# Query features on eight array tiles, kv and key features on four, whole-row loads on one queue, and a new order of the first and the last chunk of a sketched attention with a two-layer block behind it

## The chip, the cores and the metric

One core of a Trainium2 chip runs the whole kernel. The metric is the time of the device in microseconds. Engines are named as in the profile: PE (TensorE; PEld its weight loads), DVE (VectorE), ACT (ScalarE), POOL (GpSimd) and SP (SyncE, which here only issues DMAs).

## The reference

The inputs are q, k, v of shape (4, 4, 1088, 32) in float32 (batch, head, row, width), two sketches S1 and S2 of shape (8, 32), and for the second block g_ln (128), w_ch1 (128, 512) and w_ch2 (512, 128). S1, S2, w_ch1 and w_ch2 are float64.

```python
def phi(x):                                  # 64 features of a row of 32
    a, b = S1 @ x, S2 @ x                    # 8 each
    return outer(a, b)
kv  = sum over s of phi(k)[s, f] * v[s, d]   # 64 x 32 for each batch and head
z   = sum over s of phi(k)[s, f]
att = (phi(q) @ kv) / (phi(q) @ z + 1e-06)
x   = the four heads side by side            # (4, 1088, 128)
xn  = (x - mean(x)) / sqrt(var(x) + 1e-06) * g_ln
out = x + max(xn @ w_ch1, 0) @ w_ch2
```

## The kernel before

All matmuls are in float32. The work is cut into nine chunks. Chunks 0 to 7 are halves of a batch, four tiles of 128 rows each; chunk 8 (`LAST`) gathers the 64 rows left over from each of the four batches, two tiles. The order of all instructions is written out by hand: each engine runs its own instructions in program order, so what stands where in the code sets the queues. All eight PSUM banks are named by number.

**Loads** (lines 100 to 143). K and Q of batch 0 come in parts (`load_rows` with a part), V of batch 0 by four loads and two small ones on ACT's queue, w1, g, w2 and everything later on SP's.

**Start** (184 to 220). Twelve matmuls of an identity with itself run on PE (191). `hm` and `hp2` are masks of ones and zeros by head. S1 and S2 are turned into float32 on DVE (`rounded`, 146, the same routine that takes a float64 weight apart into a main and a rest term: an absolute value on ACT (163), a clamp on POOL (164), four steps on DVE (169 to 174)), laid out four times side by side (213) and transposed on PE into bank 7 (217). From that come `sk` (485), 128 x 64, which holds S1 and S2 for each head on the head's own 32 partitions, and `wb` and `wa` (494), 128 x 128, for two heads at a time.

**Keys of a batch.** `key_rows` (240) transposes K on DVE in 32 x 32 blocks, in three parts (four tiles, four tiles, 64 rows). `key_features` (259) multiplies by `sk` on PE: the stationary operand is 64 rows of K at a time, so two column tiles of the array. ACT copies the result (269), and `key_products` (271) forms the 64 products of each row and head, mostly on POOL, for batch 0 in part on DVE. `key_tokens` (248) copies V beside a column of ones, which makes z a column of kv. `key_values` (283) sums phi(k) times V over nine tiles on PE, per tile four matmuls with 64 columns in the stationary operand and 33 to stream; two ACT copies (297) lay the four heads' results out in `kvz`, block by block over two heads, zeros between, which POOL writes in `fill` (222).

**Queries of a chunk.** `query_rows` (304) transposes Q on DVE. `query_features` (317) runs, for each half of the chunk, `wb` and `wa` against Q for two pairs of heads: a row tile of 64 partitions for each pair, 128 columns in the stationary operand, 256 to stream. ACT copies one factor (333), DVE multiplies the other by it (337) into `qp`. `numerators` (343) multiplies `qp` by `kvz`, 64 rows of the output at a time (32 in chunk 8), two heads at once, 66 columns to stream; DVE adds 1e-6, takes the reciprocal and multiplies (364 to 369) for each half.

**Second block.** `statistics` (379) takes mean and variance on DVE and POOL, `root` (403) the inverse root on ACT, DVE and POOL, `turn_x` (419) transposes x on PE into bank 7 with an ACT copy (427). `hidden` (429) is one quarter of the first layer: a matmul with 512 columns to stream into bank 4 or 5, then the maximum with 0 on ACT (437). `second` (439) is the second layer into bank 6, `result` (450) scales and adds on DVE (457) and stores. The first layer's weight is made on the chip: `center` (512) takes mean and g_ln into it, and `first_weight` (475) multiplies, one half of w1 at a time.

**The loop** (529). In iteration c: the four quarters of the first layer of chunk c; the inverse root of c; numerators and statistics of c + 1; in every second iteration the kv products of the next batch, in the others its key features and key products; the second layer of c; the turning of x of c + 1; the result of c; the query features of c + 2. Iteration 0 differs: the query features of chunk 1, the keys of batch 1 and the preparation of w2 stand there (534 to 545), with the statistics of chunk 0 behind POOL's key products, and the numerators of chunk 1 behind the second layer. In the last iteration the two tiles are taken one after the other, second layer and result, both through bank 6 (563 to 567).

## Time and profile before

| what | value |
|---|---|
| time, median of 3 runs | 142.17 us (141.99 to 142.64) |
| the profiled execution's own time | 142.8 us |
| its span, first to last instruction | 140.9 us |
| mean granted clock of PE | 0.949 |
| busy: PE / DVE / ACT / POOL | 122.1 / 62.7 / 46.0 / 45.7 us |
| instructions in all, of them PE matmuls | 3109, 1259 |

A float32 matmul of the program stands in the profile as two matmul instructions and two weight loads. Matmuls are pipelined and their ends are modelled, so the chain of waits, which gives each instruction only the time until the next one could follow, is the better measure of what a group of them costs. "x16" is a count of instructions. In the chain, "issue" is time in which an engine waited for nothing that the profile shows; ACTq or SPq is the queue of an engine that issues DMAs. A group's last part is the idle time before it and what ended it.

### The profile page before, as it was taken

The numbers are of one execution on the slowest core, as the hardware profiler recorded it, in microseconds if no ns is written. First come the engines' busy times: TensorE is split into PE (matmuls) and PEld (weight loads), VectorE is DVE, ScalarE is ACT, GpSimd is POOL, SyncE is SP. The second block draws the span as 40 slices with busy tenths as digits, with TensorE's granted clock in tenths as the row PEclk, the third lists the DMA queues.
The fourth block names the chain that finished last, engine by engine and source line by source line (L and its number), as shares of the span: only waits on it lengthen the run. The fifth ranks groups of instructions, "written<-read, shape, count | busy, mean of one in ns | idle before, by whom it ended". The sixth has DMA issues, their size and how long they took to land.

```text
span 140.9 us, 3109 instructions
## 1 busy us (share of the span) xinstructions
PE 122.1 (87%) x1259; PEld 90.9 (65%) x1259; DVE 62.7 (45%) x194; ACT 46.0 (33%) x100; POOL 45.7 (32%) x139
## 2 busy tenths in 40 slices
PE   6966751995399799999999999999999999999861
PEld 6955631454399555983897399479839938839650
DVE  2359553507402834733525583334336435513310
ACT  0048112275000236226214631631362263161320
POOL 5007503005797520592270039423002302304020
PEclk9999995599869869999999999999999999999998
DMA  2999989980000011002100200110020020011021
GB/s 63 245 285 352 243 265 230 305 219 0 2 0 5 0 38 39 5 0 44 37 0 7 65 7 0 27 52 0 5 56 19 0 45 34 2 34 41 6 59 51
DMA packets 8782, 10.17 MB, mean 72 GB/s; under 512 B 2112, under 2 KB 6848, under 8 KB 8768
## 3 DMA queue, kind: packets, MB, share of 16 engines
q1 hardware_dynamic: 7888, 9.41, 26.0%
q10 hardware_dynamic: 880, 0.56, 1.8%
q8 instruction: 10, 0.16, 0.5%
q14 instruction: 4, 0.03, 0.1%
HBM read 7.74 MB, written 2.23 MB: 71 GB/s over the span
## 4 chain that ended last, share of the span: by engine, by line
PE 69%; DMA 8%; POOL 8%; DVE 5%; issue 4%; ACT 2%; SPq 1%; POOLq 0%; ACTq 0%
PE banks L434 23%; PE banks L443 20%; PE banks L328 11%; PE banks L358 6%; DMA qn<-in_q_dram 4%; DMA vn<-in_v_dram 4%; POOL kp L276 3%; PE banks L290 3%; PE banks L425 2%; PE banks L479 2%; POOL cl L164 2%; PE banks L264 2%; POOL v L257 1%; SPq L106 1%; DVE x L369 1%
## 5 line engine op out<-in xcount | busy, mean ns | idle before, releaser
L443 PE MATMUL banks<-w,hT 128*128 128x128 f32 x272 | 34.6, 287 | 4.6 <-POOL w L541 3.3
L443 PEld LDWEIGHTS banks<-w,hT 128*128 128x128 f32 x272 | 32.9, 200 | 5.4 <-POOL w L541 3.4
L434 PE MATMUL banks<-xT,w 128*128 128x512 f32 (+1 forms) x72 | 33.3, 604 | 0.5 <-ACT xT L427 0.5
L437 ACT ACTIVATE hT<-banks 128x512 f32<-128x512 f32 (+1 forms) x36 | 20.7, 574 | 12.4 <-PE banks L434 12.3
L434 PEld LDWEIGHTS banks<-xT,w 128*128 128x128 f32 x72 | 12.0, 194 | 18.2 <-ACT hT L437 10.2
L276 POOL TENSOR_TENSOR kp<-fs 128x1024 f32<-128x1024 f32 (+1 forms) x10 | 16.1, 1628 | 8.4 <-ACT fs L269 8.4
L337 DVE TENSOR_TENSOR qp<-banks,qb 128x512 f32<-128x512 f32 x17 | 11.6, 689 | 15.2 <-ACT qb L333 15.2
L412 POOL TENSOR_TENSOR r<-va,r 128x4 f32<-128x4 f32 (+1 forms) x9 | 1.8, 200 | 50.7 <-DVE den L364 46.2
L457 DVE SCALAR_TENSOR_TENSOR ob<-banks,rstd,x 128x128 f32<-128x128 f32 x34 | 9.7, 343 | 18.3 <-PE banks L443 6.9
L427 ACT COPY xT<-banks 128x512 f32<-128x512 f32 (+1 forms) x9 | 5.1, 563 | 29.1 <-PE banks L425 29.1
L411 DVE RECIPROCAL r<-r 128x4 f32<-128x4 f32 (+1 forms) x9 | 1.6, 176 | 29.1 <-ACT r L407 29.1
L328 PE MATMUL banks<-qT,wb 64*128 64x256 f32 x68 | 12.0, 432 | 1.8 <-DVE qT L233 1.0
L333 ACT COPY qb<-banks 128x512 f32<-128x512 f32 x17 | 9.9, 586 | 8.4 <-PE banks L328 8.4
L358 PEld LDWEIGHTS banks<-kvz,qp 128*64 128x64 f32 (+1 forms) x288 | 8.7, 134 | 6.1 <-issue 5.3
L328 PE MATMUL banks<-qT,wa 64*128 64x256 f32 x68 | 11.1, 406 | 0.0
L290 PE MATMUL banks<-v,kp 128*64 128x33 f32 (+1 forms) x288 | 9.7, 223 | 1.2 <-POOL kp L276 0.6
L358 PE MATMUL banks<-kvz,qp 128*64 128x66 f32 (+1 forms) x288 | 9.9, 224 | 0.6 <-ACT kvz L297 0.6
L290 PEld LDWEIGHTS banks<-v,kp 128*64 128x64 f32 (+1 forms) x288 | 9.2, 137 | 1.8 <-issue 0.9
L328 PEld LDWEIGHTS banks<-qT,wb 64*128 64x128 f32 x68 | 6.2, 197 | 4.4 <-issue 1.8
L164 POOL TENSOR_SCALAR cl<-cl 128x256 f32<-128x256 f32 (+1 forms) x3 | 4.1, 1355 | 14.2 <-ACT cl L163 14.1
L328 PEld LDWEIGHTS banks<-qT,wa 64*128 64x128 f32 x68 | 7.2, 204 | 1.0
L369 DVE TENSOR_TENSOR x<-banks,rden 128x256 f32<-128x256 f32 x17 | 7.2, 424 | 0.6
(66 smaller groups left out, 111.0 us busy)
## 6 DMA issues: line engine op xcount, KB each, us to landing
out_dram<-ob SPq DMA_DIRECT2D x8, 256.0 KB
kn<-in_k_dram SPq DMA_DIRECT2D x3, 544.0 KB
qn<-in_q_dram SPq DMA_DIRECT2D x3, 544.0 KB
vn<-in_v_dram SPq DMA_DIRECT2D x12, 128.0 KB
w_raw<-in_moe_w_ch_dram SPq DMA_DIRECT2D x2, 512.0 KB
kn<-in_k_dram SPq DMA_DIRECT2D x2, 256.0 KB
vn<-in_v_dram ACTq DMA_DIRECT2D x4, 128.0 KB
qn<-in_q_dram SPq DMA_DIRECT2D x2, 256.0 KB
```

Of the source, the lines that this page charges most:

```text
L164: eng.tensor_scalar(out=size, in0=size, scalar1=2.0**-15, scalar2=_f32_of(0x47EFFFFF), op0=ALU.max, op1=ALU.min,)
L276: eng.tensor_tensor(out=_ap(kp, 0, m, t0 * H * F, [[F, tiles * H], [R, R], [1, R]]), in0=_ap(fs, 0, m, 0, [[R2, tiles * H], [1, R], [0, R] ...
L290: nc.tensor.matmul(kvp[F * (h % 2) : F * (h % 2) + F, D1 * (h // 2) : D1 * (h // 2 + 1)], kp[0:m, H * F * t + F * h : H * F * t + F * (h + ...
L328: nc.tensor.matmul(bank(2 * i2 + pair)[:, o : o + 256], w[rows, :], qT[rows, 256 * i2 : 256 * i2 + 256], start=True, stop=True,)
L333: nc.scalar.copy(_ap(qb, 0, P, 0, two), _ap(banks, 0, P, 1024 * i2, [[512, 2], [1, 256]]))
L337: nc.vector.tensor_tensor(out=_ap(p, 0, P, 0, two), in0=_ap(banks, 0, P, 1024 * i2 + 256, [[512, 2], [1, 256]]), in1=_ap(qb, 0, P, 0, two) ...
L358: nc.tensor.matmul(nd[u : u + step, o : o + 2 * D1], qp[:, t : t + step], kvz[:, 2 * D1 * pair : 2 * D1 * (pair + 1)], start=True, stop=True,)
L369: nc.vector.tensor_tensor(out=_ap(x, 0, P, 256 * i2, [[D, 2 * H], [1, D]]), in0=_ap(nd, 0, P, 0, [[D1, 2 * H], [1, D]]), in1=_ap(rden, 0, ...
L434: nc.tensor.matmul(hp[:, 0:n], w1[:, P * j : P * (j + 1)], xTs[c][:, 0:n], start=True, stop=True)
L437: nc.scalar.activation(hTs[c][:, 512 * j : 512 * j + n], hp[:, 0:n], AF.Relu)
L443: nc.tensor.matmul(po[:, DM * i : DM * (i + 1)], hT[:, 512 * j + P * i : 512 * j + P * i + P], w2[:, DM * j : DM * (j + 1)], start=(j == 0 ...
L457: nc.vector.scalar_tensor_tensor(out=ob[:, t], in0=po[:, t], scalar=rstd[:, i : i + 1], in1=x[:, t], op0=ALU.mult, op1=ALU.add,)
```

## The change

Loads: K and Q of every batch come as whole rows (4,352 bytes per partition), all on SP's queue; V of batch 0 goes from ACT's queue to SP's, behind Q of batch 0 and ahead of w1.

Array tiles: the query features work on 32 partitions (one head) and 64 columns (`wa`, `wb` without the mask), both halves of the chunk and all four heads in turn: 16 matmuls for 8. Key features take 32 rows of K in the stationary operand for 64, and the kv products 32 columns for 64: twice the matmuls each. The numerators follow the new layout: one head, 64 partitions, 33 columns to stream, 32 matmuls for 16. `kvz` loses its zeros and `fill` the writing of them; ACT makes four copies for two. DVE's denominators of a chunk are taken together.

Order of the first chunk: six warm-up matmuls for twelve; `wa` and `wb` are copied by ACT; part 1 of V's copies goes from ACT to POOL; both clamps of w1 stand ahead of `center`, w1's second half is multiplied between the second and third quarter of the first layer (bank 7); w2's clamp stands ahead of the loop; the statistics of chunk 0 go ahead of POOL's key products, and the copies of V ahead of the product of each part; the root of chunk 0 goes ahead of the second layer. In the last chunk the root stands ahead of the first layer, and the two tiles have a bank each.

```diff
-    load_rows(kn, k, 0, 0)
-    load_v(0, nc.scalar, False)
-    load_rows(kn, k, 0, 1)
-    load_rows(qn, q, 0, 0)
+    load_rows(kn, k, 0)
+    load_rows(qn, q, 0)
+    load_v(0, nc.sync, False)
+    load_v(0, nc.sync, True)
     nc.sync.dma_start(out=w1_raw, in_=moe_w_ch1)
-    load_v(0, nc.scalar, True)
...
-    for i in range(12):
+    for i in range(6):
         nc.tensor.matmul(bank(i % 2)[:, 0:P], ident, ident, start=True, stop=True)
...
     def key_features(b, part, at):
-            for u in range(0, m, 64):
+            for u in range(0, m, 32):
                 nc.tensor.matmul(
-                    kf[u : u + 64, 64 * i : 64 * i + 64],
-                    kT[:, P * i + u : P * i + u + 64], sk, start=True, stop=True,
+                    kf[u : u + 32, 64 * i : 64 * i + 64],
+                    kT[:, P * i + u : P * i + u + 32], sk, start=True, stop=True,
                 )
...
     def key_values(b, at):
-            for h in range(H):
+            for i in range(2 * H):
+                h, o = i // 2, 32 * (i % 4)
                 nc.tensor.matmul(
-                    kvp[F * (h % 2) : F * (h % 2) + F, D1 * (h // 2) : D1 * (h // 2 + 1)],
-                    kp[0:m, H * F * t + F * h : H * F * t + F * (h + 1)],
+                    kvp[o : o + 32, D1 * (h // 2) : D1 * (h // 2 + 1)],
+                    kp[0:m, H * F * t + 32 * i : H * F * t + 32 * i + 32],
                     v1[0:m, W * t + D1 * h : W * t + D1 * (h + 1)],
...
     def query_features(c):
-        for i2 in range(ntiles(c) // 2):
-            for o, w in ((0, wb), (256, wa)):
-                for pair in range(2):
-                    rows = slice(64 * pair, 64 * pair + 64)
+        for o, w in ((0, wb), (256, wa)):
+            for half in range(2):
+                for h in range(H):
+                    rows = slice(D * h, D * h + D)
                     nc.tensor.matmul(
-                        bank(2 * i2 + pair)[:, o : o + 256],
-                        w[rows, :], qT[rows, 256 * i2 : 256 * i2 + 256], start=True, stop=True,
+                        bank(h)[F * half : F * half + F, o : o + n], w[rows, :],
+                        qT[rows, n * half : n * half + n], start=True, stop=True,
                     )
...
     def numerators(c):
+        for i in range(n):
+            for h in range(H):
+                for half in range(2):
+                    rows = slice(F * half, F * half + F)
                     for u in range(0, P, step):
                         kvz = kvzs[CHUNKS[c][0] if c < LAST else u // 32]
+                        t, o = 256 * h + P * i + u, W * i + D1 * h
                         nc.tensor.matmul(
+                            bank(half)[u : u + step, o : o + D1], qp[rows, t : t + step],
+                            kvz[rows, D1 * h : D1 * h + D1], start=True, stop=True,
                         )
...
+    def second_at(c, i):
+        return bank(6)[:, DM * i : DM * (i + 1)] if c < LAST else bank(6 + i)[:, 0:DM]
...
     for c in range(LAST + 1):
         b = c // 2 + 1
+        if c == LAST:
+            root(c)
         for j in range(JC):
+            if (c, j) == (0, 2):
+                first_weight(1)
             hidden(c, j)
         if c == 0:
-            next(w2_steps)
             query_features(1)
             for part in range(3):
-                key_features(1, part, (6, 7, 3)[part])
+                key_features(1, part, (6, 7, 5)[part])
...
+            statistics(0)
             for part in range(3):
+                key_tokens(1, part, nc.gpsimd)
                 key_products(1, part, nc.gpsimd)
-                key_tokens(1, part, nc.gpsimd)
-            statistics(0)
-        root(c)
+            root(0)
+            second(0)
+            numerators(1)
+            key_values(1, 3)
...
```

## Rows read from the trace of the kernel before

**Rows 1.** Page, part 4: the chain that ended last, share of the span by engine.

```profile
PE 69%; DMA 8%; POOL 8%; DVE 5%; issue 4%; ACT 2%; SPq 1%; POOLq 0%; ACTq 0%
```

**Rows 2.** Chain in order of time, to chunk 1: start us, length us, what.

```profile
22.17 1.07 POOL cl L164
...
26.14 4.29 PE banks L434 x8
...
42.87 0.23 POOL v L257
...
44.25 0.21 POOL va L400
...
47.86 3.67 PE banks L328 x16
51.52 3.73 PE banks L434 x8
```

**Rows 3.** The same chain, steady part and last chunk: one row of each kind.

```profile
81.69 0.93 PE banks L264 x32
...
87.16 1.93 PE banks L328 x16
...
92.82 1.09 PE banks L358 x32
93.90 2.19 PE banks L290 x72
...
122.20 1.06 PE banks L328 x8
...
126.99 0.61 PE banks L358 x32
```

**Rows 4.** Timeline to 20 us: start us, length us, engine, line, what; idle before.

```profile
1.34 7.68 ACTq L116 DMA_DIRECT2D vn<-in_v_dram  x6
1.34 5.49 PE L192 MATMUL banks<-ident 128*128 128x128 f32 x24 [1.34 <-POOL ident masks.py:199]
...
3.91 0.28 DVE L213 TENSOR_TENSOR s<-up,rest 16x128 f32<-16x128 f32 x1
...
5.31 0.71 DVE L233 STREAM_TRANSPOSE kT<-kn 128x512 f32<-128x512 f32 x1 [1.13 <-DMA kn<-in_k_dram]
...
9.05 1.28 ACT L186 ACT_TABLE_LOAD   x1 [9.05 <-DMA qn<-in_q_dram]
...
11.17 2.72 POOL L276 TENSOR_TENSOR kp<-fs 128x1024 f32<-128x1024 f32 x1 [8.36 <-ACT fs L269]
...
19.86 0.70 PE L479 MATMUL banks<-rest,center 128*128 128x256 f32 x2
```

**Rows 5.** Page, part 2: GB/s of all DMA in 40 slices of 3.52 us.

```profile
GB/s 63 245 285 352 243 265 230 305 219 0 2 0 5 0 38 39 5 0 44 37 0 7 65 7 0 27 52 0 5 56 19 0 45 34 2 34 41 6 59 51
```

**Rows 6.** Groups by line and form: busy us, mean ns of one; idle before.

```profile
L257 POOL COPY v<-vn 128x512 f32<-128x512 f32 x6 | 3.6, 613 | 0.0
...
L297 ACT COPY kvz<-banks 64x66 f32<-64x66 f32 x8 | 1.7, 210 | 8.7 <-PE banks L290 6.7 <-POOL center L512 1.9
...
L164 POOL TENSOR_SCALAR cl<-cl 128x256 f32<-128x256 f32 x2 | 2.1, 1075 | 5.7 <-ACT cl L163 5.7
...
L163 ACT ACTIVATE cl<-w_raw 128x256 f32<-128x256 f32 x2 | 0.9, 439 | 0.0
```

**Rows 7.** Windows: length, busy of PE, PEld, DVE, ACT, POOL; granted clock; DMA.

```profile
16.70:18.26 1.56, 0.45 (x16) 0.31 (x12) 1.40 (x6) 0.00 (x0) 0.00 (x0) 1.00 0.99 305
20.56:21.76 1.20, 0.57 (x4) 0.19 (x2) 0.00 (x0) 0.96 (x3) 0.00 (x0) 0.57 1.10 235
20.70:27.50 6.80, 3.86 (x9) 2.12 (x8) 3.37 (x8) 1.55 (x4) 1.06 (x1) 0.50 1.08 268
```

**Rows 8.** Timeline of the end: start us, length us, engine, line; idle before.

```profile
136.60 1.16 PE L443 MATMUL banks<-w,hT 128*128 128x128 f32 x8 [1.29 <-DVE ob L457]
137.80 0.35 DVE L457 SCALAR_TENSOR_TENSOR ob<-banks,rstd,x 128x128 f32<-128x128 f32 x1 [1.25 <-PE banks L443]
```

More of the change, by code (lines that the diff above doesn't have):

```diff
@@ L98, with load_rows @@
     w2_raw = raw_tile([P, JC * DM], moe_w_ch2, "w2_raw")
-    def load_rows(t, src, b, part=None):
-        base = src.offset + b * H * S * D
-        cuts = {None: [(0, [[1, G * D]])], 0: [(0, [[256, 4], [1, 128]])],
-                1: [(128, [[256, 4], [1, 128]]), (1024, [[1, 64]])]}
-        for o, free in cuts[part]:
-            nc.sync.dma_start(
-                out=_ap(t[b], 0, P, o, free),
-                in_=bass.AP(src.tensor, base + o, [[G * D, P]] + free),
-            )
+    def load_rows(t, src, b):
+        nc.sync.dma_start(
+            out=t[b], in_=bass.AP(src.tensor, src.offset + b * H * S * D, [[G * D, P], [1, G * D]])
+        )
     def load_v(b, eng, rest):
@@ L296, in key_values @@
         for i in range(2):
-            nc.scalar.copy(
-                _ap(kvz, F * i, F, D1 * i, [[2 * D1, 2], [1, D1]]),
-                _ap(kvp, F * i, F, 0, [[D1, 2], [1, D1]]),
-            )
-    qTs, qps, xs, rs, mvs, xTs, hTs, obs = {}, {}, {}, {}, {}, {}, {}, {}
+            for to in range(2):
+                nc.scalar.copy(
+                    _ap(kvz, F * to, F, D1 * i, [[2 * D1, 2], [1, D1]]),
+                    _ap(kvp, F * i, F, 0, [[D1, 2], [1, D1]]),
+                )
+    qTs, qps, xs, rs, mvs, xTs, hTs = {}, {}, {}, {}, {}, {}, {}
     def query_rows(c):
@@ L363, in numerators @@
-            rden = small.tile([P, 2 * H], F32, tag="rden", name="rden")
-            nc.vector.tensor_scalar(
-                out=den, in0=_ap(nd, 0, P, D, [[D1, 2 * H]]),
-                scalar1=1e-6, scalar2=None, op0=ALU.add,
-            )
-            nc.vector.reciprocal(rden, den)
+                            bank(half)[u : u + step, o : o + D1], qp[rows, t : t + step],
+                            kvz[rows, D1 * h : D1 * h + D1], start=True, stop=True,
+                        )
+        den = small.tile([P, 4 * H], F32, tag="den", name="den")
@@ L369, in numerators @@
+        rden = small.tile([P, 4 * H], F32, tag="rden", name="rden")
+        m = n * H
+        nc.vector.tensor_scalar(
+            out=_ap(den, 0, P, 0, [[m, 2], [1, m]]),
+            in0=_ap(banks, 0, P, D, [[512, 2], [D1, m]]),
+            scalar1=1e-6, scalar2=None, op0=ALU.add,
+        )
+        nc.vector.reciprocal(rden[:, 0 : 2 * m], den[:, 0 : 2 * m])
+        for half in range(2):
             nc.vector.tensor_tensor(
-                out=_ap(x, 0, P, 256 * i2, [[D, 2 * H], [1, D]]),
@@ L371, in numerators @@
-                in0=_ap(nd, 0, P, 0, [[D1, 2 * H], [1, D]]),
-                in1=_ap(rden, 0, P, 0, [[1, 2 * H], [0, D]]),
+                out=_ap(x, 0, P, D * m * half, [[D, m], [1, D]]),
+                in0=_ap(banks, 0, P, 512 * half, [[D1, m], [1, D]]),
+                in1=_ap(rden, 0, P, m * half, [[1, m], [0, D]]),
                 op=ALU.mult,
@@ L475, in first_weight @@
     def first_weight(i):
-        w1p, terms = bank(4 + i), next(w1_steps[i])
+        w1p, terms = bank((4, 7)[i]), w1_terms[i]
         for j, term in enumerate(terms):
@@ L487 @@
     )
+    for w, o, pat in ((wb, R, [[0, R], [1, R]]), (wa, 0, [[1, R], [0, R]])):
+        nc.scalar.copy(_ap(w, 0, P, 0, [[R, R], [1, R]]), _ap(sp, 0, P, o, pat))
     key_rows(0, 1)
@@ L556 @@
                 key_products(b + 1, part, nc.gpsimd)
-        if c < LAST:
-            second(c, 0, 4)
-        if c == 0:
-            numerators(1)
-            statistics(1)
-            key_values(1, 3)
-        if c == LAST:
-            for i in range(ntiles(c)):
-                second(c, i, i + 1)
-                result(c, i, i + 1)
-            break
+        if c > 0:
+            second(c)
         turn_x(c + 1)
         query_rows(c + 2)
-        result(c, 0, 4)
+        result(c)
         query_features(c + 2)
```

112 lines of the change are left out of this document (47 added, 65 removed).

## The prediction

> **What bounds the kernel now.** I read the chain of waits that ended last first. TensorE (PE) carries 69% of it [rows 1], but the rest is not spread evenly. The same chain in order of time splits the span in two. Up to 51.52 us, where the hidden layer of chunk 1 starts, it hops between DMA, POOL, DVE and PE [rows 2]; from there to the numerators of the last chunk at 126.99 us [rows 3] it is PE alone. So the start must be read for what comes late, and the middle for what PE spends. In the middle one chunk is made of the pieces of [rows 3]: query features 1.93 us (16 instructions; each f32 matmul shows as two, so eight matmuls), numerators 1.09 (32 instructions), in every second chunk key features 0.93 for the two full parts and kv products 2.19 (72 instructions); the hidden layer is 3.73 [rows 2]. The rows of the start [rows 4] show why the first 26 us hold so little: ACT issues six loads of v until 9.02 us and only then its table load of 1.28 us, so the copy of the key features, and POOL's key product behind it, begin at 11.17; and PE is in its 24 warm-up instructions until 6.83 us, though S, which is to be transposed, is ready at 4.19 us.
>
> **The change part by part.** I sum against the profiled execution: span 140.9 us and 1.9 us around it, 142.8 us. That run is 0.6 us above the median of 142.17, so 0.6 us comes off at the end.
>
> *A, to the first hidden layer* (starts at 26.14 us [rows 2]). The change takes v off ACT's queue and puts K, Q and V of batch 0 ahead of w1 on SP's. By the rates of the page (63, then 245, 285 and 352 GB/s in slices of 3.52 us [rows 5]) the whole K of 544 KB is in by 4.9 us, Q by 7.1, V by 9.1, w1 by about 10.9, and K, V and Q of batch 1 by 17.9, before DVE comes to them; whole rows may go faster, and S, ready at 4.19 us, is the bound from below. SP issues now what ACT did: even at ACT's 7.68 us for six loads w1's turn comes before 10, ahead of its data. With half the warm-up instructions PE is free by about 4.1 us. DVE loses two products for the query weights to ACT, where two short copies (0.21 us each by the nearest row [rows 6]) lie beside DVE's transposes. From K: two transposes of 0.71 us on DVE with the small product between, the features of part 1 on PE, ACT's copy: POOL's key product starts near 7.4 us instead of 11.17 and ends at 10.1 if it takes its 2.72 us again [rows 4]. Then come on POOL the copies of v, which the change moves to it, 0.61 us [rows 6] and 0.23 us [rows 2]: 11.0. Two branches leave here. POOL's two clamps of w1, now both ahead of the centring, end at 10.9 + 0.44 + 2 x 1.075 [rows 6] = 13.5, and the first half of w1 on PE (2 x 0.70 [rows 4]) is done by about 15.4, then 1.2 us for turning x and copying it [rows 7]. The other: kv products end near 11.4, four copies of kv where two were, 4 x 0.21 [rows 6] = 0.84, numerators 1.09 at full clock and 2.2 at half, DVE's chain to x at most 1.40 and again the 1.2 [rows 7]: 15.9 to 17.0. Between 16 and 17 by both, and each step has a short wait; I take 17.0. **A: -9.1 us.** What hides behind this: before, the second half of w1 (clamp at 22.17 [rows 2]) held up the first hidden layer; now it is multiplied between the second and third quarter of that layer, out of the way of x.
>
> *B, from there to the hidden layer of chunk 1.* Before: 4.29 us of hidden layer, then 21.1 us to 51.52 [rows 2]. The layer now contains the second half of w1: 3.73 + 1.4 = 5.1 us at full clock, 10.2 at half. The windows show granted clock 0.50 from 20.70 to 27.50 us [rows 7], after a stretch in which PE worked in bits; the new start is as broken, so I take 6.4, a quarter of it more than at full clock: +2.1. Of the 21.1 us: the query features of chunk 1 shrink by 0.8; POOL's statistics of chunk 0, 1.36 us from the end of the v copy at 43.10 to 44.46, go ahead of the key products, +1.36. Clamping w2 earlier brings nothing by itself: DVE's rounding waits behind its query products anyway. After POOL's last key product stood 8.4 us (43.10 to 51.52): statistics, root, DVE's reciprocal with the numerators of chunk 1 queued behind it, turning x, transposing Q, 3.67 us of query features at half clock. The new order does all but the last ahead of or beside the key products, because root's input is there before them; what is left is the last kv tile, four copies 0.84 us, and the query features, 1.07 to 2.0 us: 2.8. So +2.1 - 0.8 + 1.36 - 8.4 + 2.8: **B: -2.9 us.** The new bound of this stage is POOL: three key products and three copies in one row; two waiters for it are the root's POOL steps, needed only by the result of chunk 0, and the kv products.
>
> *C, the steady part.* Query features: 16 matmuls of 32 rows and 64 columns instead of eight of 64 and 128, all with 256 columns to stream, 32 instructions. Before, two tiles work at a time: 16 instructions in eight steps of about 0.214 us and a lead of 0.2 us make the 1.93. Over eight tiles 32 instructions make four steps: 0.86 + 0.2 = 1.07 us. The trace has no eight tiles; four column tiles at once it has, in the last chunk's numerators, 32 instructions in 0.61 us where two tiles need 1.09 [rows 3]. Bounds: 1.07, and 1.93 if only four work at a time. I take 1.07, as two and four tiles both scale. Five chunks give 5 x 0.86, the last (1.06 now) 0.43: -4.7. Kv products: 144 instructions on four column tiles. At the 19 ns each of the last numerators (0.61/32) they take 2.7 us, at twice the pace of now 1.1; I take 1.3, since those numerators stream 66 columns and these 33: two batches, -1.8. Numerators: 64 instructions, half the rows and half the columns each, four tiles instead of two: unchanged at 1.09, at 19 ns 1.2. Key features: twice the instructions on twice the tiles: unchanged. ACT's two more copies of kv (0.42 us), the wider denominators on DVE and the zeroing that goes from POOL are beside PE and cost nothing: the hidden layer of 3.73 us covers them, and without it each would be its own length once per chunk. The transposed x is copied while PE has the query features; 1.07 us covers the copy, half of the 1.2 us [rows 7], still. **C: -6.5 us.**
>
> *D, the end.* The second layer's matmuls of the last chunk's second half begin at 136.60, 1.29 us after PE was free, because DVE reads the bank that they write [rows 8]; with a bank for each half and the root taken ahead of the hidden layer, they follow at once, without the lead of a new start (0.1), and the last 0.35 us on DVE moves with them: **D: -1.4 us.**
>
> Sum: -9.1 - 2.9 - 6.5 - 1.4 = -19.9; 142.8 - 19.9 - 0.6 = **122.3 us**.
>
> A rule speaks against splitting small matmuls further. The row first: the last numerators start an instruction every 19 ns on average [rows 3]. The Trainium skill ("TensorE: Matmul & The Clock Gate", section "Wait — 56ns, not 53.3ns?") says that start-to-start never falls below about 25 ns however few columns are streamed. By that rule (estimate) kv products would take 144 x 25 ns = 3.6 us, numerators 1.6, and the sum would be about 133 us. The row is below the rule's figure, so it does not hold for separate tiles here.
>
> **The rivals.** (1) *A half-cold start.* The clock stays at half through the first two layers and POOL's products are stretched again, as 2.72 us shows. First layer 10.2 instead of 6.4, numerators and first weight about 1.5 more, the rest in POOL's waits: +6, 128 us. For it: the clock rows. Against: dense matmuls from 17 us on. (2) *Four tiles at a time* in the query features, so 1.93 stays: +4.7 in C, +1 in the start: 128 us. For it: no row has row and column tiles at once, nor four row tiles. (3) *A fixed spacing of instructions*: if the 29 to 34 ns per instruction seen in key features, kv products and numerators belong to the instruction and not to its columns, doubling their number doubles them: kv products 4.4, numerators 2.2, key features +0.9 each time: +15 in C, +2 in the start, 139 us. Against: 19 ns in the last chunk; with 19 ns throughout it is only 126. (4) *Slower: row tiles of 32 do not overlap at all.* 32 instructions one after the other at 0.214 us, with the lead 7.0 us per chunk, 5.9 over the forecast: +33 us in C (5.5 chunks) and, of 18 for the three chunks of the start, perhaps 15: about 170 us. It decides from 3.7 us per chunk on, where the 15 us of A, B, D and the kv products are used up over 8.5 chunks, that is with fewer than two tiles at once. Against: row tiles of 64 overlap fully now.
>
> **How the numbers follow.** Chances: forecast 0.56 (117 to 126), half-cold start 0.17, four tiles 0.11, spacing 0.08, slower 0.05, mixtures that cancel to within 0.5% (what a measurement here can tell from no change, 0.7 us) 0.03. The range from 116.5 takes in the start at full clock (-2.5), K landing early (-0.7) and kv products at 1.1 with the copies hidden (-2); to 129.5 it takes in rivals 1 and 2. Outside lie most of 3, 4 and some tails, under 0.2. Faster 0.92, same 0.03, slower 0.05.
>
> **What would show it.** Right: ACT's table load before 3 us, POOL's first key product near 7.4, the first hidden layer near 17, that of chunk 1 near 39; query features 1.1 us, kv products 1.3, numerators 1.1; the chain PE alone after 39. Wrong: query features at 1.9 or above (2, 4), kv products above 2.7 (3), the first hidden layer after 22 (1), or DVE or ACT in the chain after 45, which would mean that the shorter query features no longer cover the copies.

## The result, and the profile after the change

| | before | after |
|---|---|---|
| median | 142.33 us (141.99 to 142.64) | 136.04 us (135.00 to 136.64) |
| ratio, 95% interval | | 0.955 (0.949 to 0.962) |
| profiled execution: own time, span | 142.8, 140.9 us | 135.0, 133.2 us |
| A: start to first hidden layer | 26.14 | 20.99 (-5.2; forecast -9.1) |
| B: from there to hidden layer of chunk 1 | 25.38 | 23.10 (-2.3; forecast -2.9) |
| C: from there to hidden layer of chunk 8 | 80.52 | 80.63 (+0.1; forecast -6.5) |
| D: from there to the end of the span | 8.88 | 8.48 (-0.4; forecast -1.4) |

Faster, by 6.3 us, but only a third of what was forecast and above the range given. The four parts are differences of starts in the chain of waits. Ratios here and below leave disturbed executions out (one of them, of the kernel with key features on two tiles again, took 189.98 us at a granted clock of 0.563). The four misses add up to some 12 us; what the median misses beyond that is the 0.6 that the forecast took off and that the profiled execution was the fastest of its four. C gained nothing at all.

The chain of the changed kernel, three pieces of the start and then the steady part (start us, length us, what):

```profile
12.26 1.61 issue
...
15.05 2.41 PE banks L348 x64
17.46 2.00 PE banks L471 x4
...
47.82 1.07 PE banks L348 x64
...
54.48 1.05 PE banks L319 x32
...
60.32 1.15 PE banks L280 x103
61.46 1.93 issue
...
85.45 1.44 PE banks L280 x129
86.89 1.92 issue
89.07 5.40 PE banks L440 x32
```

In the steady part query features (L319) take 1.05 us where [rows 3] had 1.93, numerators (L348) 1.07 for twice the instructions: as forecast. The new thing is "issue": PE stands still for 1.9 us in the middle of the kv products (L280), and after the second stop the second layer (L440) takes 5.40 us instead of 3.77. The waits of PE name no engine behind it (engine, line, what it waited for: total us, times, longest):

```profile
PE banks L280 <- issue: 5.5, 3, 1.9
PE banks L440 <- POOL w L535: 4.5, 1, 4.5
```

The third stop is in the start, at 12.26 us. The windows (length, PE busy, granted clock, DMA share, GB/s) show what the stops leave behind:

```profile
14.00:20.83 6.83, 5.99 (x107) 0.50 0.84 227
...
61.50:63.40 1.90, 0.01 (x1) 1.00 0.00 0
89.10:92.51 3.41, 3.41 (x17) 0.50 0.02 5
```

Nothing runs on PE from 61.50 to 63.40. Behind the stops at 12.26 and 86.89 the granted clock is 0.50 (1.2 GHz in place of 2.4), behind the one at 61.46 it stays at 1.00 until 89.10. And one row of the page's part 3 (queue: packets, MB, share) has grown, from 10 packets and 0.16 MB before to:

```profile
q8 instruction: 16, 0.26, 0.9%
```

These are fetches of instructions, 16,384 bytes each. PE now has 2,111 matmul instructions for 1,259, and as many weight loads. The stops come before matmul instructions 222, 1115 and 1626 in PE's order, counted from 0. Let a place be the position in PE's stream with the loads counted too: these are places 444, 2230 and 3252, and their distances are 7 x 256 - 6 and 4 x 256 - 2. So the theory to be tested, **P**: PE's stream comes in pages of 256 places, a page that is used up too soon makes PE wait for the next. Numerators and kv products pass 416 places in 2.5 us. By the packets' records the fetches behind the two steady stops start 0.8 and 0.7 us after the page ahead of the stop was begun and take 1.3 and 1.2 us, and PE goes on 1.3 and 1.4 us after they have landed: 3.4 and 3.3 us from border to border, where the work of such a page is 1.4 to 1.5.

### The profile page after: what moved, and what is told of

Same layout as the page of the kernel before. It is cut to its first block, busy times and chain, and to the rows that moved or that the text cites. A ratio compares the mean times of both kernels' runs of the same rounds, so it can differ in the third digit from the quotient of the medians.

```text
span 133.2 us, 4803 instructions
## 1 busy us (share of the span) xinstructions
PE 112.3 (84%) x2111; PEld 82.2 (62%) x2111; DVE 58.0 (44%) x178; ACT 46.4 (35%) x110; POOL 44.3 (33%) x131
## 4 chain that ended last, share of the span: by engine, by line
PE 75%; issue 6%; DVE 5%; DMA 4%; SPq 3%; ACT 3%; POOL 1%; ACTq 0%; POOLq 0%
PE banks L440 27%; PE banks L427 24%; PE banks L348 8%; PE banks L319 6%; PE banks L280 4%; DMA vn<-in_v_dram 4%; PE banks L418 3%; SPq L110 2%; PE banks L471 2%; PE banks L249 1%; ACT xT L420 1%; POOL w L535 1%; DVE qp L328 1%; SPq L101 1%; DVE st L379 1%
## 5 line engine op out<-in xcount | busy, mean ns | idle before, releaser
L440 PE MATMUL banks<-w,hT 128*128 128x128 f32 x272 | 36.7, 299 | 4.5 <-POOL w L535 4.5
L440 PEld LDWEIGHTS banks<-w,hT 128*128 128x128 f32 x272 | 35.2, 212 | 5.1 <-POOL w L535 4.7
L328 DVE TENSOR_TENSOR qp<-banks,qb 128x512 f32<-128x512 f32 (+1 forms) x18 | 11.1, 657 | 13.5 <-ACT qb L327 13.5
L348 PEld LDWEIGHTS banks<-kvz,qp 64*64 64x64 f32 (+1 forms) x576 | 10.1, 140 | 5.9 <-issue 3.8
L280 PE MATMUL banks<-v,kp 128*32 128x33 f32 (+1 forms) x576 | 7.4, 200 | 5.7 <-issue 5.5
L348 PE MATMUL banks<-kvz,qp 64*64 64x33 f32 (+1 forms) x576 | 11.1, 227 | 0.3 <-ACT kvz L288 0.3
L327 ACT COPY qb<-banks 128x512 f32<-128x512 f32 (+1 forms) x18 | 9.2, 565 | 4.3 <-PE banks L319 3.3
L280 PEld LDWEIGHTS banks<-v,kp 128*32 128x32 f32 (+1 forms) x576 | 6.3, 110 | 7.2 <-issue 6.5
L249 PE MATMUL banks<-sk,kT 128*32 128x64 f32 x272 | 6.1, 244 | 2.2 <-DVE sk L477 2.2
L379 DVE BATCH_NORM_STATS2 st<-x 128x6 f32<-128x128 f32 x34 | 7.4, 278 | 0.0
L319 PE MATMUL banks<-qT,wb 32*64 32x256 f32 (+1 forms) x144 | 6.4, 416 | 0.7 <-DVE qT L218 0.7
L362 DVE TENSOR_TENSOR x<-banks,rden 128x256 f32<-128x256 f32 (+1 forms) x18 | 6.5, 405 | 0.3
## 6 DMA issues: line engine op xcount, KB each, us to landing
vn<-in_v_dram SPq DMA_DIRECT2D x16, 128.0 KB
out_dram<-ob SPq DMA_DIRECT2D x1, 128.0 KB
```

The costliest lines, as they stand in the source:

```text
L249: nc.tensor.matmul(kf[u : u + 32, 64 * i : 64 * i + 64], kT[:, P * i + u : P * i + u + 32], sk, start=True, stop=True,)
L280: nc.tensor.matmul(kvp[o : o + 32, D1 * (h // 2) : D1 * (h // 2 + 1)], kp[0:m, H * F * t + 32 * i : H * F * t + 32 * i + 32], v1[0:m, W * ...
L319: nc.tensor.matmul(bank(h)[F * half : F * half + F, o : o + n], w[rows, :], qT[rows, n * half : n * half + n], start=True, stop=True,)
L327: nc.scalar.copy(own, _ap(banks, 0, P, 512 * h, [[512, 2], [1, n]]))
L328: nc.vector.tensor_tensor(out=_ap(p, 0, P, 256 * h, [[256, 2], [1, n]]), in0=_ap(banks, 0, P, 512 * h + 256, [[512, 2], [1, n]]), in1=own, ...
L348: nc.tensor.matmul(bank(half)[u : u + step, o : o + D1], qp[rows, t : t + step], kvz[rows, D1 * h : D1 * h + D1], start=True, stop=True,)
```

## The experiments

Rivals of P were **W**, a wait on another engine that belongs to the new products and that the trace does not name, and **T**, that products on four tiles are slow in themselves. Chunk intervals below go from one hidden layer's start to the next; 2 to 3 and 4 to 5 hold the kv products of batches 2 and 3 (from the first matmul, within 0.1 us of the chain).

| kernel | median us | 2 to 3 | 4 to 5 | 1 to 8 |
|---|---|---|---|---|
| before | 142.3 | 13.14 | 13.14 | 80.6 |
| after | 136.04 | 13.70 | 15.30 | 80.7 |
| kv on two tiles | 133.14 | 12.39 | 12.39 | 76.5 |
| 128 places more at the start | 136.32 | 11.54 | 12.45 | 76.4 |
| kv dealt out | 135.07 | 12.40 | 12.40 | 76.5 |
| before, kv on four tiles | 144.89 | 13.74 | 12.43 | 80.5 |
| 32 places more in chunk 1 | 131.62 | 12.27 | 11.53 | 76.0 |
| 128 places more in chunk 1 | 137.27 | 14.81 | 15.10 | 84.2 |
| kv in two lots | 129.44 | 11.70 | 11.70 | 76.3 |

**Kv products back on two column tiles** (the loop over eight pieces of 32 columns becomes one over four of 64).

```diff
-            for i in range(2 * H):
-                h, o = i // 2, 32 * (i % 4)
+            for h in range(H):
...
```

> The changed kernel with the kv products back on two column tiles (144 instructions and 144 weight loads' worth halved to 72 and 72 per batch). Theory P (pages): TensorE's instructions arrive in pages of 256, and a page that is used up in under about 3.4 us lets PE wait for the next; the three idle pieces of 1.6, 1.9 and 1.9 us in the kv products are that. It expects the pieces gone or under 0.5 us, the second layer after the kv products of batch 3 back from 5.40 to 3.77 us, kv products 2.2 us each, and 132 to 133 us in all. Theory W (a wait that the profile doesn't show, for POOL's key product or the copy of v): the pieces stay, 1.6 to 1.9 us, and with slower kv products the time rises to 137. Theory T (four column tiles with accumulation stall of themselves): gone too, 132 to 133 us, so this run separates W alone.

133.14 us (132.45 to 133.94), ratio to before 0.939 (0.931 to 0.946). Its chain has no stop in the steady part:

```profile
62.41 2.34 PE banks L279 x72
64.75 3.77 PE banks L439 x32
```

Products of 2.34 us beat products of 1.7 (1.44 and 0.26) with a stop of 1.9. Undoing this one part gives back 4.2 us of the stretch.

**The same program, 128 places later.** 32 small idle matmuls (nobody reads their results) behind the turning of S.

```diff
+    for i in range(32):
+        u = 32 * (i % 4)
+        nc.tensor.matmul(bank(0)[u : u + 32, 0:64], ident[:, 0:32], ident[:, 0:64], start=True, stop=True)
     sk = consts.tile([P, H * R2], F32, name="sk")
```

> The changed kernel with 32 small matmuls more (64 instructions and 64 weight loads, so 128 places in PE's stream) in a stretch where PE is idle, behind the transpose of S. Theory P: the idle pieces move by 128 places towards the front: in the kv products of batch 2 from the 118th of 144 instructions to about the 54th, in batch 3 from the 137th to about the 73rd, 1 to 2 us each; total within 1.5 us of the changed kernel either way. Theories W and T: the pieces stay at the 118th and 137th instruction, total unchanged but for up to 1 us in the start.

Nearly the same median (136.32), but the stops moved in the program and not in the stream:

```profile
65.93 1.49 PE banks L283 x139
67.42 3.77 PE banks L443 x32
...
88.90 0.76 PE banks L283 x68
89.66 0.70 issue
90.36 0.94 PE banks L283 x67
```

Batch 3 stops earlier in its products, again before matmul instruction 1626, and the one in the start again before 222. A wait for an operand would have moved with the operand. W falls. The expectation was wrong for batch 2, which runs through in 1.49 us: the page ahead of its border now takes in the hidden layer and lasts 5.6 us. And two stops are new, 2.61 us in the numerators of chunk 0 (before matmul instruction 349) and 1.37 in the kv products of batch 1 (before 732): further borders of the same count.

**The products of batches 2 and 3 dealt out between the tiles of the second layer** (three tiles of keys behind each of the first three).

```diff
         for i in range(ntiles(c)):
+            if b is not None and 0 < i:
+                key_values(b, 3, range(3 * i - 3, 3 * i))
```

> The changed kernel, same instructions and same tiles, but the kv products of batches 2 and 3 dealt out in three parts between the four output tiles of the second layer. Theory P: a page now lasts 3 us or more, the idle pieces shrink from 1.9 to under 0.5 us each and the second layer of chunk 4 keeps its full clock: 131 to 133 us. Theory T: the idle pieces stay, split or whole, 135 to 136 us. Theory W: they vanish, as the products come later.

No stop, and no gain over two tiles:

```profile
64.50 1.09 PE banks L443 x8
65.59 0.56 PE banks L278 x44
...
68.89 0.65 PE banks L278 x48
69.54 1.09 PE banks L443 x8
```

Seven such pieces make 6.13 us, where the lumped two-tile form has 2.34 + 3.77 = 6.11. A second layer cut in four costs 4.36 for 3.77, and 0.56 us per 48 instructions is 12 ns each for 10: going over from the products to the second layer costs about 0.15 us a time, which with the slower pieces is all that four tiles give. T holds for this order, not for the products in one row. The total says little here, its four executions lie between 127.33 and 136.79 us; the profiled one, of 134.98, stands still for 4.68 us in the start, again before matmul instruction 222.

**The kernel before with kv on four tiles alone.**

> The kernel before with one part of the change alone: the kv products on four column tiles. Its numerators have 64 instructions and 64 loads, half of the changed kernel's. Theory P: 288 places in some 1.4 us hold a whole page, so idle pieces of 1 to 2 us turn up in or right behind the kv products of batches 2 and 3 in this kernel too, and the time goes from 142.3 to between 141.5 and 146. Without the page limit (W) the kv products take 1.4 us where they took 2.2 and the time falls by 1.5 to 2.5 us, to about 140.3.

Slower: 144.89, ratio 1.019 (1.009 to 1.029). The stop of batch 2 lies right behind the products here, where the border falls:

```profile
69.07 1.49 PE banks L291 x138
70.56 1.34 issue
71.90 3.73 PE banks L444 x32
```

In batch 3 no border is in the way, and the interval is 12.43 for 13.14: 0.7 us of the 0.9 a batch of the forecast. What the one batch gains the other loses (1 to 8: 80.5 for 80.6); the rise of the median is not explained by that. The profiled execution, the fastest (143.15), stops for 1.69 us in the start, before matmul instruction 221, and reaches chunk 1 0.5 us later than the kernel before; the slower three left no profile.

**Where the border falls, set on purpose.** Two kernels (warm start as below, batch 0 on two tiles) that differ in one number, the small idle matmuls in the gap between the key features of batch 2, 8 or 32.

```diff
             for part in range(3):
+                for i in range(8 if c == 1 and part == 2 else 0):
...
                 key_features(b + 1, part, 2 + part % 2)
```

> The kernel with the warm start (six warm-ups behind the turn of S, four idle 512-column matmuls in the first chunk), with the key/value products of batch 0 on two column tiles and those of batches 1 to 3 on four, and 8 small idle matmuls (32 places of TensorE's instruction stream) in the gap between the key features of batch 2. Theory P (TensorE's instructions come in pages of 256, a page lasts at least 3.4 us, and a stall is a page used up sooner): counted from the stalls of the changed kernel, the page borders now fall 180 and 218 places into the 416 places of numerators and products of batches 2 and 3, so each passes one border only: no idle piece there, products at 1.44 us where two tiles took 2.34, and from the first hidden layer of chunk 1 to that of chunk 8 74.6 us (76.4 with two tiles). Batch 1, border at 110, may stall about 1 us ahead of that stretch. Whole run about 127.5. Theory W (the pieces are a wait on another engine that belongs to the four-tile products): an idle piece of 1.9 us in batches 2 and 3 as before, the stretch 78.4 or more.

> The same with 32 small idle matmuls (128 places) in that gap instead of 8: the work, its order and its waits are those of the kernel with 8, and only the place in the stream of everything behind chunk 1 is 96 later. Theory P: the borders fall 84 and 122 places into the numerators and products of batches 2 and 3, so a second border comes 256 places on, within the 416: an idle piece of 1.5 to 2 us inside the products of both batches, the stretch from the hidden layer of chunk 1 to that of chunk 8 77.5 to 79 us, 3 to 4 above the kernel with 8, and about 131 for the whole. Theory W: the same as with 8, plus at most 0.3 us for 24 small matmuls.

With 8, 131.62 us; from its chain, batches 2 and 3:

```profile
62.07 1.49 PE banks L283 x131
63.55 1.20 PE banks L443 x9
64.75 0.58 issue
...
85.77 1.49 PE banks L283 x131
87.26 3.77 PE banks L443 x32
```

With 32, 137.27 us, ratio to before 0.957 (0.948 to 0.966) where the other has 0.921 (0.913 to 0.928):

```profile
63.23 1.03 PE banks L283 x100
64.26 1.46 issue
65.72 0.65 PE banks L283 x39
66.37 5.40 PE banks L443 x32
...
89.48 1.19 PE banks L283 x114
90.67 1.71 issue
92.39 0.51 PE banks L283 x19
92.90 5.39 PE banks L443 x32
```

24 small matmuls, 1.0 us in themselves (the group takes 0.22 us with 8, 1.18 with 32), add over 5 us, by moving what follows 96 places. Interval 4 to 5 with the border well placed is 11.53 us, 1.6 below before; badly placed 15.10, of which 1.7 is the stop and 1.6 the second layer at half clock behind it. Two details of the expectations were wrong. With 8, batch 2 still stopped, in the second layer, where the next border came 20 places behind the row; 0.7 us of it shows. And with 8 the whole was to take about 127.5 us: batch 1 stopped for 1.90 at 39.91, and the half clock behind it reached into the hidden layer of chunk 1, which began at 45.28.

**All stops together.** The traces of all kernels here have 20 idle pieces of PE over 0.5 us that are put down to "issue". They stand before matmul instructions 221 or 222 (eight kernels), 349, 603, 732, 859, 1114 or 1115 and 1626: whole steps of 127.6 matmul instructions from the first, to within two, whatever the instruction there works on, in the kernel before with four-tile products as in the others. Each ends 1.27 to 1.57 us after the end of a fetch of 16,384 bytes. So it is the supply of instructions, in the start as well. The 3.4 us are no fixed limit: in the changed kernel the page before matmul instruction 605 lasted 1.59 us without a stop, behind a second layer at half clock, with a fetch that began 2.9 us before PE reached the border ahead of it.

**The four-tile products in two lots**, tiles 0 to 4 behind the numerators, 5 to 8 behind the query features.

> Warm start, batch 0 on two tiles, and the four-tile products of batches 1 to 3 in two lots: tiles 0 to 4 behind the numerators, tiles 5 to 8 behind the query features two chunks on (bank 5 in place of bank 3), so that 288 and then 192 places pass in a row where 416 did. Theory P: hardly an idle piece whatever the place of the borders (one only if a border falls in the first 32 places of the 288), products together 1.5 to 1.8 us per batch where two tiles took 2.34, the stretch from the hidden layer of chunk 1 to that of chunk 8 74.5 to 75.2 us, and the whole 126.5 to 127.5. If the four-tile products are slow in themselves (theory T: a switch of tile shape costs what the tiles give, as when they were dealt between the second-layer tiles): the stretch stays at 76.4 or above.

129.44 us. No stop in any batch, products 0.83 and about 0.8 us. But the stretch is 76.3, not 74.8: the hidden layer behind the second lot waits for bank 5 until ACT, which has the query copies to do first, has copied kv out:

```profile
65.83 0.78 PEld L281 LDWEIGHTS banks<-v,kp 128*32 128x32 f32 x64 [0.39 <-issue]
...
66.02 1.07 ACT L331 COPY qb<-banks 128x512 f32<-128x512 f32 x2 [0.49 <-PE banks L323]
...
67.91 0.30 PEld L431 LDWEIGHTS banks<-xT,w 128*128 128x128 f32 x2 [0.96 <-ACT kvz L292]
```

**The start: the clock.** All on two-tile products. Six more warm-up matmuls behind the turning of S; then the same with two idle 512-column matmuls behind the query features and two behind the kv products of chunk 0.

> The changed kernel with kv products on two column tiles, plus the six warm-up matmuls that the change took out, set behind the transpose of S, where PE waits for K. Theory C (clock): in the changed kernels the granted clock falls to 0.50 before the numerators of chunk 0 and stays there into the first hidden layer, because PE has less to do in the first microseconds than before; with PE busy until K comes, full clock lasts from about 7 to 14 us or beyond, the numerators of chunk 0 take 1.1 to 1.3 us where they took 2.4, the first hidden layer starts 1.5 to 3 us earlier than the 21.2 us without, total 129.5 to 132 us. Rival N (the warm-ups are worth nothing; the clock falls because of the later idle stretches): the same granted clock from 12 us on, total 133 us within 0.7.

> As the run with the six warm-ups behind S's transpose, plus two idle matmuls of 512 columns behind the query features and two behind the kv products of chunk 0, whose results nobody reads, so that PE is busy where it waited for POOL and ACT. Theory C: full clock from about 7 us into the first hidden layer, which then takes 3.8 us and starts at 18 to 19.5; total 127 to 130 us. Rival N: as without them or up to 2 us slower, since the idle matmuls hold up the numerators: 133 to 135 us.

The first took 126.9 to 128.0 us in three executions (mean granted clock 0.973 to 0.986), ratio 0.893 (0.886 to 0.900); its profiled one, at 0.948, took 133.2. The second took 128.87 to 129.35, ratio 0.905 (0.899 to 0.910). Its chain, start of chunk 0:

```profile
8.46 1.12 PE banks L320 x32
9.58 1.91 PE banks L496 x4
...
13.84 1.91 PE banks L511 x4
15.75 1.07 PE banks L349 x64
16.82 1.06 PE banks L472 x4
...
19.30 1.98 PE banks L428 x4
```

The hidden layer starts at 19.30 with 2 x 1.91 us of idle work (L496, L511) ahead of it, 21.24 without in the kernel on two tiles, whose clock was at 0.50 from 8.3 to 25.3. Not all of that idle work could be left out: without it (the last run below) the kv products of chunk 0 wait for the copy of V until 10.22 and the numerators for the copies of kv until 12.94; with 1.07, 1.06, 0.77 for turning x and 0.59 for its copy behind that, the hidden layer would start at about 16.5 (an estimate from these rows), near the 17.0 forecast.

What the idle matmuls do is not settled. The profiled execution of the first kernel, of 133.2 us, kept full clock from 5.51 us on, then stopped for 2.38 us at 14.18, before matmul instruction 221, and had half clock from 15.75. In every profile with a stop of over 0.5 us there, the clock is at half behind it; the two idle pairs also make PE come to that border later, at about 16 us, when the fetch has landed (at 12.77 in the second run). Whether they help by keeping PE busy or by keeping the border out of the way was not tested. In the kernel on two tiles, without warm-ups behind S, the clock fell with no such stop.

**The old loads under the new kernel.**

> The changed kernel with kv products on two column tiles, and the loads of the kernel before: K and Q of batch 0 in parts, V of batch 0 on ACT's queue. Theory A: ACT issues loads until 9 us and only then loads its table, so the copies of the key features begin at 10.4 us, POOL's first key product at 11 instead of 8.4, and the first hidden layer starts 2 to 3 us later: 135 to 136.5 us. Rival: the key features wait for K and the clock in any case, the parts bring K earlier than the 5.7 us of whole rows, and nothing is lost: 132.5 to 133.7 us.

133.66 us, ratio 0.927 (0.918 to 0.937), against 0.939 (0.931 to 0.946) with the new ones: not told apart. The first hidden layer started at 22.82 in place of 21.24, and that of chunk 1 at 46.20 for 46.11. As theory A had it, the old loads hold up ACT's table load (8.78 us) and POOL's first key product (11.12 for 8.40). Whole rows bring the first part of K later (DVE's first transpose at 5.73 for 5.08) and the rest earlier (the query features at 8.76 for 10.43). In the profiled executions the mean granted clock was 0.974 with the old loads and 0.922 with the new ones, so they differ by more than the loads.

**Chunk 7's store by rows in four.**

```diff
-                out.tensor, out.offset + row * DM, [[step * DM, 4], [G * DM, 32], [1, n * DM]]
...
+                    out.tensor, out.offset + (row + a * step) * DM,
+                    [[step * DM, m], [G * DM, 32], [1, n * DM]],
```

> The changed kernel with kv products on two column tiles, and the store of chunk 7 (256 KB, 5.9 us from issue to the last landing, on few of the DMA engines) cut into four stores of 32 partitions each. Theory S: that store is what the last store queues behind in the changed kernel, so its end moves from 2.9 us after the last store's issue to about 1.8 us as in the kernel before, the time from the last result on DVE to the end of the span falls from 3.9 to 2.8 us, total about 1 us lower, 132.1. Rival: the last store takes 2.9 us by itself; no change in that stretch.

The changed kernel's last DVE instruction ends at 129.27, yet its span runs to 133.2; the stores' issue row:

```profile
125.23 4.44 SPq L456 DMA_DIRECT2D out_dram<-ob  x2
...
128.92 0.35 DVE L451 SCALAR_TENSOR_TENSOR ob<-banks,rstd,x 128x128 f32<-128x128 f32 x1 [0.49 <-PE banks L440]
```

By the packets' records chunk 7's 256 KB land from 126.4 to 130.8, and the last 128 KB, which share the end of that time, until 131.76: 2.5 us after their issue, where it was 1.4 before. In four pieces the 256 KB land within 1.9 us, and from the hidden layer of chunk 8 to the end it is 7.24 us (123.34 to 130.58) for 8.48. So D's gain was won on PE and DVE (6.11 us from that hidden layer to DVE's last instruction before, 4.55 now) and mostly lost again to this store. The total, 131.85 us (126.35 to 132.56), spreads too far to show it.

**A version that takes all of it.** The traces show one more wait: the second layer of chunk 0 stands 4.5 us for w2 (L535, above), whose cleaning on DVE is queued behind the query products of chunk 1, and POOL's statistics behind that. Both moved ahead of the loop:

```diff
+    up, *rest = next(w2_steps)
...
+    statistics(0)
     for c in range(LAST + 1):
```

First without the statistics, on the products in two lots and with one idle matmul at each place:

> The split products, with three more things the traces point to: the rest of the cleaning of w2 on DVE and POOL ahead of chunk 0's hidden layer (it stood behind query features of chunk 1 on DVE, and the second layer of chunk 0 waited 4.5 us for it), chunk 7's store cut by rows into four, and one idle matmul in place of each two. If the second layer of chunk 0 then starts right behind the key features of batch 1 (26.8 in the warm run, 31.3 there), POOL's products of batch 1 end near 33 in place of 38.2 and the hidden layer of chunk 1 starts near 36 (42.2): about 119 to 121 for the whole with the stretch at 74.8 and the end 1.3 shorter. If POOL's chain, not w2, sets chunk 1 (the products of batch 1 wait for values or key features instead), it gains 1.5 to 3 there and ends near 123. If one idle matmul does not keep the clock up, some 3 to 5 more.

123.98 us, ratio 0.865 (0.856 to 0.873); hidden layer of chunk 1 at 43.4 after one of chunk 0 at 21.2: in the profiled execution, the slowest of the four (128.52), PE stopped for 1.90 us before matmul instruction 221 and the clock was at half in the start again, and POOL's key products now waited for its statistics. Then with both, on two-tile products:

> Key/value products on two column tiles, the warm start with two idle matmuls at two places, chunk 7's store in four, and ahead of chunk 0's hidden layer the rest of w2's cleaning and the statistics of chunk 0 (DVE, POOL). If those two were what held the first chunk: second layer of chunk 0 at about 26.8 (31.3 in the warm run), POOL's products of batch 1 done near 32.6 (38.2), hidden layer of chunk 1 near 36 (42.2), the stretch to chunk 8 76.4 as before, about 121.5 for the whole and steady to 0.5. If the clock still falls in the first 25 us: 124 to 127.

> The same with the key features on two tiles again, as before the change (the products stay as they are). If four tiles only turn TensorE's time into a wait for ScalarE's copies of the features (0.63 and then 0.7 of waiting, where it was 0.93 and then 0.3): the same within 0.3 us, with 11.3 to 11.5 us from the hidden layer of an even chunk's predecessor to the next (11.43). If they give what the forecast's rows said of a matmul that is done sooner: 0.3 us more for each of three batches, so about 1 us longer in all.

> The same as the first without the four idle matmuls. If the clock stays up without them: hidden layer of chunk 0 at about 15.5, and the whole 2 to 4 us shorter, about 118; in runs where the clock falls while TensorE waits for loads and copies, hidden layer of chunk 0 at 21 or later and 123 to 126: times of two kinds, not a spread.

With two idle matmuls at each place 122.40 us, ratio 0.861 (0.855 to 0.868): second layer of chunk 0 at 27.64, hidden layer of chunk 1 at 37.4:

```profile
27.64 3.81 PE banks L441 x32
31.45 0.94 PE banks L349 x54
32.96 2.34 PE banks L281 x72
```

Key features on two tiles again change nothing (ratio 0.859, 0.852 to 0.867; intervals 11.47 for 11.43): PE is done 0.4 us sooner with four and then waits for ACT's copies. Without the idle matmuls three executions took 119.9 to 120.2, at a granted clock of 1.00, ratio 0.844 (0.835 to 0.853), the best of all; two others 122.6 and 126.4 at 0.986 and 0.959. The profiled one of these, of 122.6, shows a stop of 1.56 us at 14.07, again before matmul instruction 221, and half clock from 16.25 to 19.67:

```profile
12.94 1.12 PE banks L349 x24
14.07 1.56 issue
```

So to hold the clock with idle matmuls costs 2.2 us here, and not to hold it up to 6.

## Why the prediction was wrong

**C failed at one term, and not at the one that was doubted.** The step was "I take 1.3 [...] two batches, -1.8" for the kv products. Their pace was nearly right (1.49 us where nothing stops them), and so were the query features (1.05 for 1.07) and the numerators (1.07). What it left out is that an instruction must first be there: the working counted instructions by their duration only, and the change took PE's matmul instructions from 1,259 to 2,111. The two intervals with kv products should have come to 2 x 11.4 us (13.14, less 0.86 and 0.9); with a border well placed they are 11.53, and as they stood 13.70 and 15.30: two stops of 1.9 us, 1.6 of half clock behind one of them, and 0.2 for each new start. With every border well placed the stretch would be 11.43 + 11.53 + 11.43 + 11.53 + 10.05 + 9.80 + 8.99 = 74.8, an estimate from the intervals above: -5.8, near the -6.5. Of the 0.7 left, 0.3 is the two intervals with products (1.61 gained in each for 1.76; the row takes 1.49 us for 1.3); 0.16 is the two intervals with key features (0.78 gained for 0.86), where PE now waits for ACT's copies; the rest is the last two chunks, where the cover of the copy of x is gone (0.60 us of ACT stand in the chain at chunk 7). The text foresaw that cover and took it to hold.

**A failed at the same missing term, and at the clock.** Its order of events was right: the table load ends at 2.6 us, the first query features come at 8.7, the clamps at 12.3 to 14.4. But "numerators 1.09 at full clock and 2.2 at half", with 17.0 taken between, let the clock cost about 1 us; the stop cost 1.6, and half clock 2.3 (numerators 2.41 for 1.07, first weight 2.00 for the 1.06 of the run with idle matmuls). POOL's first product began at 9.10 for 7.4, because K landed at 5.77 and not by 4.9, and the key features took 2.13 us (1.37 in the kernel with products on two tiles); the product itself took 1.95 us for the 2.72 expected. (One edit is not in the list of the change: DVE's key products of batch 0 read one factor from PSUM. The two took 1.51 us, 3.32 before.) Rival 1, the half-cold start, was the nearest: it put 6 us on the start. Without the stop and at full clock some 16.5 us would have stood in place of the 17.0 (the estimate above).

**B** was nearly right (-2.3 for -2.9), by cancelling: the second layer of chunk 0 waited for w2 for 4.5 us, which B did not price though it named the queue ("DVE's rounding waits behind its query products anyway"), and took 6.18 us for 3.77 behind that wait, at a granted clock of 0.50 from 31.07 to 37.90; against that, the first hidden layer with the second half of w1 took 5.3 us for the 6.4 taken. Moving the wait out is worth about as much: with the statistics, 5.3 us from the first hidden layer to that of chunk 1 (22.85 in the run with idle matmuls, 17.57 with both moved).

**D** had the mechanism right (the second layers follow at once) and the end wrong: before, chunk 7's store had landed at 138.15, ahead of the last one's issue (138.18); now it is still landing when DVE is done (129.27), and the last store, which shares the time with it, sets the end. The working followed PE and DVE and stopped at their last instruction.

**Rivals.** Four tiles at a time and row tiles that do not overlap are out (1.05 us). Rival 3, a spacing that belongs to the instruction, came true in another form: not so many ns for each, which 1.49 us for 144 exclude (10 ns), but so many us for a page of 256 places, 3.3 and 3.4 at the two steady stops. The 133 us that the rule of 25 ns gave lies nearer to the result than the forecast, by another cause.

## What to carry to other kernels

Cutting matmuls into more array tiles multiplies instructions, and where some hundreds pass in a few us their supply becomes the bound: look for idle time put down to "issue" on PE and for more packets in the instruction queue, count places between the stops, and use fewer, larger tiles or put slow matmuls between the fast rows. Here only the first paid: no kernel with four-tile products came below 76.0 us from chunk 1 to 8, and two tiles give 76.5 wherever the borders fall; the 74.8 is an estimate that no run reached. Such a stop costs twice when the clock falls behind it. A stretch of this kind can be good or bad by 3.5 us with the alignment alone, so a neutral edit far ahead of it may seem to cost or to give microseconds.

## What was not expected of the hardware

- Stops of PE at fixed places of its instruction stream, 256 apart: 0.6 to 1.9 us from the kv products of batch 1 on, 4.7 us in the start of the dealt-out kernel, where loads fill the DMA engines (265 GB/s during the stop). The Trainium skill ("Runtime: NRT & Kernel Launch", section "Instruction fetch mechanics") describes the blocks of 16 KiB and 256 instructions that the runs show, and says that crossing one is mostly hidden. Here it is not, where a page is used up in 1.4 to 1.5 us: the two steady stops are 1.9 us each.
- Matmuls of 33 columns on four column tiles follow each other at 10 ns (144 in 1.49 us). "TensorE: Matmul & The Clock Gate", section "Wait — 56ns, not 53.3ns?", of the Trainium skill has about 25 ns as a floor; on separate tiles it does not hold here.
- Going over on PE from the 32-column products to the 128-column second layer costs about 0.15 us (the second layer cut in four: 4.36 for 3.77).
- One store of 256 KB in four groups of 32 partitions took 4.4 us to land, the last of it beside the last store (4.4 in the kernel before too, alone), the same bytes as four stores 1.9 us. By the records such a store ends with 4 packets of 4 bytes, each of the four pieces with 16.
